# K and V pairs loaded with the two batches on separate partition halves, and three V pairs kept instead of two

## Chip, cores, metric

One core of a Trainium2 chip. The metric is the device time of one execution in microseconds. Executions of one kernel agree within about 1% (the four of the kernel before: 185.68 to 186.6 us). The ratios and intervals are from fast runs in the same rounds on the same chip, so a ratio is not quite that of the medians quoted beside it. A difference counts as faster or slower only when it is clear of 2%.

## The reference

A decode step: one token for each of 4 batches, twice through an attention layer and a gated feed-forward layer, with the same weights and the same cache both times.

```python
x = x + A(layernorm(x)); x = x + B(layernorm(x))     # and both once more

# A: 32 query heads, 8 K/V heads of 128, the last W = 2048 cached positions
q = (x @ wq) per head; scores = q . k * Dh**-0.5; p = softmax(scores); o = p . v; o @ wo
# B: h = sigmoid(x @ w_gate) * (x @ w_up); h @ w_down
```

Everything is bfloat16. The window of K is 16.8 MB (4 batches x 8 heads x 2048 x 128 x 2 bytes), and that of V as much. K stays in on-chip memory for the second attention. V doesn't fit and is read twice, except for what is kept.

## The kernel before

The program is made from a plan: every operation states what it reads and writes, a scheduler orders them, and all transfers from DRAM are issued in order by SyncE. The on-chip arena has 50 slots of 4 KB per partition. A tile is two slots (1 MB): 16 tiles hold all of K, nine are free for V and weights. A "pair" is one head's K or V of two batches. These are the parts that matter (cut):

```python
KEEP_V = cfg.get("KEEP_V", 2)      # V pairs not read again; one of them is parked in PSUM

def pair_d(cache, h, bp):          # the DRAM side of one pair's load: 64 rows, 2 batches, 8 KB
    return cache[2 * bp:2 * bp + 2, h, SK - W:SK, :].rearrange("b (p j) d -> p b (j d)", p=64)

# scores: 32x32 blocks of the K tile are transposed in place by VectorE, so the batch of a
# column is its parity: 16 columns of one batch, every second 4-byte word
kt = kpair(hk, b // 2).rearrange("p (j c x i t) -> p c t i j x", c=2, x=16, i=2, t=2)
pe.matmul(ps[32 * gi:32 * gi + NR, bank, :], qbd[...], kt[:, cp // 2, cp % 2, b % 2, :, :], ...)
```

With this order, partition 2p holds row p of the pair's first batch and partition 2p + 1 that of the second: the batches are interleaved over the partitions.

## Time and profile before

| | before |
|---|---|
| time, median | 186.48 us |
| bytes moved, mean rate | 72.12 MB, 391 GB/s |
| packets' time as a share of 16 DMA engines | 97.2% |
| TensorE busy | 55% |

From the page of the kernel before: the share of DMA busy time in 40 equal slices of the span (9 is 90% or more), the rate in each slice, the packet counts, the main load queue (packets, MB, share of 16 engines), the chain of waits by engine, and two groups of matmuls (line, engine, operation, output <- inputs, shapes, count | busy us, mean ns | idle before, releaser).

```profile
DMA  5999999999999999999999999999999999999980
GB/s 198 425 427 427 425 403 391 411 421 419 409 387 425 419 421 403 392 419 419 400 391 414 412 407 393 403 350 417 330 396 419 419 423 416 418 416 402 412 341 24
DMA packets 15379, 72.12 MB, mean 391 GB/s; under 512 B 1144, under 2 KB 5248, under 8 KB 8704
...
q1 hardware_dynamic: 15352, 71.84, 97.2%
...
DMA 52%; PE 25%; SPq 16%; DVE 4%; issue 2%; ACT 0%
...
L697 PE MATMUL ps<-arena,qbd 128*16 128x512 bf16 x256 | 32.5, 626 | 16.9 <-DVE qbd L668 8.4 <-DVE arena L678 7.5 <-issue 1.0
...
L726 PE MATMUL ps<-prow,perm 64*128 64x256 bf16 x64 | 7.4, 315 | 2.4 <-ACT prow L714 2.3
```

The DMA engines are full from the second slice to the 38th. By this page the kernel is bound by the bytes it reads (experiment 4 shows where that reading ends). One small number is worth more than it seems: "under 512 B 1144". No load of this kernel has rows that short. In the trace they are packets of four bytes. The input x and the output have four data packets each, and with them four of these, one at the end of each data packet (3 or 4 ns before it). The count of all is 71 large loads x 16 + 4 for the four-row output + 4 for the four-row input x = 1144. I read one as the mark of one DMA engine's end of a transfer (an interpretation). Read this way, the page tells how many engines each load used.

The views of single stretches give the second attention (129 to 165 us) 405 GB/s, with a chain of TensorE pieces. TensorE is busy for 33.6 of these 36 us, and the DMA share is 1.01.

### The profile page before, as it was taken

The numbers are of one execution on the slowest core, as the hardware profiler recorded it, in microseconds if no ns is written. First come the engines' busy times: TensorE is split into PE (matmuls) and PEld (weight loads), VectorE is DVE, ScalarE is ACT, GpSimd is POOL, SyncE is SP. The second block draws the span as 40 slices with busy tenths as digits, with TensorE's granted clock in tenths as the row PEclk, the third lists the DMA queues.
The fourth block names the chain that finished last, engine by engine and source line by source line (L and its number), as shares of the span: only waits on it lengthen the run. The fifth ranks groups of instructions, "written<-read, shape, count | busy, mean of one in ns | idle before, by whom it ended". The sixth has DMA issues, their size and how long they took to land.

```text
span 184.4 us, 4421 instructions
## 1 busy us (share of the span) xinstructions
PE 101.2 (55%) x1944; PEld 54.7 (30%) x1944; DVE 89.5 (49%) x221; ACT 35.7 (19%) x100; POOL 14.8 (8%) x77
## 2 busy tenths in 40 slices
PE   0532423652807327173373545445979997994474
PEld 0101000332303323023232441210334653584422
DVE  5209998477592565925621531138463442340330
ACT  2003022240212103011020001001365442220010
POOL 4000000110000101010010000000022111120000
PEclk9999995585766756755555555555897897885569
DMA  5999999999999999999999999999999999999980
GB/s 198 425 427 427 425 403 391 411 421 419 409 387 425 419 421 403 392 419 419 400 391 414 412 407 393 403 350 417 330 396 419 419 423 416 418 416 402 412 341 24
DMA packets 15379, 72.12 MB, mean 391 GB/s; under 512 B 1144, under 2 KB 5248, under 8 KB 8704
## 3 DMA queue, kind: packets, MB, share of 16 engines
q1 hardware_dynamic: 15352, 71.84, 97.2%
q8 instruction: 15, 0.25, 0.5%
q14 instruction: 4, 0.03, 0.0%
q10 hardware_dynamic: 8, 0.00, 0.0%
HBM read 71.83 MB, written 0.00 MB: 390 GB/s over the span
## 4 chain that ended last, share of the span: by engine, by line
DMA 52%; PE 25%; SPq 16%; DVE 4%; issue 2%; ACT 0%
DMA arena<-in_A_v_cache_dram 33%; SPq L382 16%; PE ps L697 11%; DMA arena<-in_B_w_down_dram 9%; PE ps L770 8%; DMA arena<-in_A_wq_dram 5%; DMA arena<-in_B_w_up_dram 5%; PE ps L726 2%; PE ps L794 1%; DVE ps L492 1%; PE ps L626 1%; DVE nmax L705 1%; PE ps L749 1%; PE ps L905 1%; PE ps L852 1%
## 5 line engine op out<-in xcount | busy, mean ns | idle before, releaser
L770 PE MATMUL ps<-ebuf,arena 128*128 128x8 bf16 x1024 | 31.0, 167 | 29.7 <-DMA arena<-in_A_v_cache_dram 22.1
L697 PE MATMUL ps<-arena,qbd 128*16 128x512 bf16 x256 | 32.5, 626 | 16.9 <-DVE qbd L668 8.4
L770 PEld LDWEIGHTS ps<-ebuf,arena 128*128 128x128 bf16 x1024 | 28.8, 101 | 36.3 <-DMA arena<-in_A_v_cache_dram 32.5
L678 DVE STREAM_TRANSPOSE arena<-arena 128x1024 f32<-128x1024 f32 x32 | 37.9, 1219 | 3.3 <-DMA arena<-in_A_k_cache_dram 3.0
L705 DVE TENSOR_REDUCE nmax<-ps 128x1 f32<-128x512 f32 x16 | 11.0, 687 | 26.0 <-PE ps L697 26.0
L714 ACT ACTIVATE prow<-ps,nmax 128x512 bf16<-128x512 f32 x16 | 11.0, 687 | 39.6 <-DVE nmax L711 24.9
L671 ACT COPY qbd<-qrep 32x64 bf16<-32x64 bf16 x32 | 7.7, 241 | 40.9 <-PE ps L697 40.3
L697 PEld LDWEIGHTS ps<-arena,qbd 128*16 128x16 bf16 x256 | 6.1, 97 | 31.3 <-issue 22.0
L739 POOL CAST s<-psm 128x1 bf16<-128x1 f32 x16 | 3.0, 188 | 144.4 <-ACT prow L714 144.4
L778 DVE TENSOR_TENSOR onb<-ps,rinv 128x16 bf16<-128x16 f32 x16 | 2.9, 184 | 21.1 <-PE ps L770 21.1
L626 PE MATMUL ps<-arena,xn 128*4 128x512 bf16 x64 | 7.8, 582 | 7.6 <-DMA arena<-in_A_wq_dram 6.2
L794 PE MATMUL ps<-onb,arena 128*128 128x4 bf16 x256 | 9.1, 166 | 3.1 <-DVE onb L778 3.1
L731 ACT CAST prow<-ps 128x512 bf16<-128x512 f32 x16 | 9.4, 587 | 7.1 <-PE ps L726 7.0
L735 DVE STREAM_TRANSPOSE ebuf<-prow 128x256 f32<-128x256 f32 x16 | 7.0, 437 | 6.7 <-ACT prow L731 6.4
L852 PE MATMUL ps<-arena,xn 128*4 128x448 bf16 x64 | 6.5, 560 | 4.9 <-DVE xn L607 3.1
L794 PEld LDWEIGHTS ps<-onb,arena 128*128 128x128 bf16 x256 | 7.9, 101 | 4.1 <-DVE onb L778 2.8
L726 PE MATMUL ps<-prow,perm 64*128 64x256 bf16 x64 | 7.4, 315 | 2.4 <-ACT prow L714 2.3
L596 ACT ACTIVATE lnv<-lnv 128x4 f32<-128x4 f32 x4 | 0.8, 205 | 34.0 <-DVE lnv L593 34.0
L634 DVE STREAM_TRANSPOSE ebuf<-ps 128x512 f32<-128x512 f32 x4 | 2.9, 715 | 7.7 <-PE ps L626 7.6
L859 DVE STREAM_TRANSPOSE ebuf<-ps 128x448 f32<-128x448 f32 x4 | 2.6, 650 | 7.8 <-PE ps L852 7.8
L668 DVE COPY qbd<-qrep 32x64 bf16<-32x64 bf16 x32 | 5.3, 166 | 0.7 <-ACT qrep L657 0.2
L749 PE MATMUL ps<-sel_b,s 128*128 128x16 bf16 x48 | 3.8, 175 | 3.2 <-POOL s L743 2.4
(61 smaller groups left out, 68.1 us busy)
## 6 DMA issues: line engine op xcount, KB each, us to landing
arena<-in_A_v_cache_dram SPq DMA_DIRECT2D x30, 1024.0 KB, 16.8
arena<-in_A_k_cache_dram SPq DMA_DIRECT2D x16, 1024.0 KB, 16.0
arena<-in_A_wq_dram SPq DMA_DIRECT2D x8, 1024.0 KB, 9.4
arena<-in_A_wo_dram SPq DMA_DIRECT2D x4, 1024.0 KB, 24.3
arena<-in_B_w_gate_dram SPq DMA_DIRECT2D x4, 896.0 KB, 19.7
arena<-in_B_w_up_dram SPq DMA_DIRECT2D x4, 896.0 KB, 15.8
arena<-in_B_w_down_dram SPq DMA_DIRECT2D x2, 1024.0 KB, 12.5
arena<-in_B_w_down_dram SPq DMA_DIRECT2D x1, 768.0 KB, 7.0
```

The source lines that it names most:

```text
L382: o = P.op("sync", name, 0.0, lambda e, dst=dst, src=src: e.dma_start(dst, src), r=r, w=w, dma_bytes=nbytes, dma_rate=tm[rate])
L626: last = pe.matmul(ps[32 * hh:32 * hh + NB, qb, :], xn[:, c * NB:(c + 1) * NB], tile_ap(s)[:, o + hh * 512:o + (hh + 1) * 512], start=(c = ...
L671: P.op("scalar", "qe%s_%d" % (tag, a), c_act(64), lambda s_, dst=dst, src=src: s_.copy(dst, src), r=rd, w=[("q", k2, a)])
L678: P.op("vector", "T%d_%d" % (h, t), c_dve(1024), lambda v, v32=v32: v.transpose(v32, v32), r=[("slot", 4 * h + t)], w=[("slot", 4 * h + t)])
L697: last = pe.matmul(ps[32 * gi:32 * gi + NR, bank, :], qbd[:, q0:q0 + NR], kt[:, cp // 2, cp % 2, b % 2, :, :], start=(cp == 0), stop=(cp = ...
L705: lambda v: v.tensor_reduce(nmax[:, k2:k2 + 1], ps[:, bank, :], AXX, ALU.max),
L714: lambda a: a.activation(prow[:, :].rearrange("p (m x t) -> p m x t", x=16, t=2), ps[:, bank, :].rearrange("p (m t x) -> p m x t", x=16, t ...
L726: last = pe.matmul(ps[:, PBS[i], 0:256], perm[64 * i:64 * i + 64, jh * 128:(jh + 1) * 128], prow[64 * i:64 * i + 64, jh * 256:(jh + 1) * 2 ...
L731: lambda a: a.copy(prow[:, :].rearrange("p (y i t) -> p i y t", i=2, t=2), ps[:, PBS[0]:PBS[0] + 2, 0:256].rearrange("p i (y t) -> p i y t ...
L770: last = pe.matmul(ps[:, ob, bp * 8:bp * 8 + 8], src[:, j * 128:(j + 1) * 128], ev[:, j % 2, j % 16 // 2, x0:x0 + 8], start=(j == 0), stop ...
L794: last = pe.matmul(ps[:, WB, c * NB:(c + 1) * NB], tile_ap(s)[:, o + r_ * D + c * 128:o + r_ * D + (c + 1) * 128], ov[:, r_ * NB:(r_ + 1) ...
L852: last = pe.matmul(ps[32 * g:32 * g + NB, OBS[n], 0:NF], xn[:, c * NB:(c + 1) * NB], tile_ap(s)[:, o:o + NF], start=(c == 0), stop=(c == N ...
```

## The change

The intent: with the batches of a pair on separate partition halves, one score matmul serves both batches (half of the keys at a time) and reads every second bf16 instead of every fourth; the matrices that sort the probabilities become one 128x128 permutation; and a third V pair stays for the second attention, which saves one load of 1 MB. The core of the diff, with cuts marked:

```diff
-    KEEP_V = cfg.get("KEEP_V", 2)
+    KEEP_V = cfg.get("KEEP_V", 3)
 ...
         def pair_d(cache, h, bp):
-            return cache[2 * bp:2 * bp + 2, h, SK - W:SK, :].rearrange("b (p j) d -> p b (j d)", p=64)
+            return cache[2 * bp:2 * bp + 2, h, SK - W:SK, :].rearrange("b (p j) d -> b p (j d)", p=64)
 ...  (scores; still 16 matmuls of 512 columns per head)
-                        kt = kpair(hk, b // 2).rearrange("p (j c x i t) -> p c t i j x", c=2, x=16, i=2, t=2)
+                        kt = kpair(hk, bp).rearrange("p (j c x t) -> p c t j x", c=2, x=32, t=2)
 ...  (the maximum now has to cross the two halves)
+            for g in range(2):
+                P.op("vector", "nx%d%s" % (g, tag), tm["dve_small"],
+                     lambda v, g=g: v.tensor_copy(nmax[64 * g:64 * g + 64, 4 + k2:5 + k2],
+                                                  nmax[64 - 64 * g:128 - 64 * g, k2:k2 + 1]), ...)
 ...  (sorting the probabilities: four matmuls become one)
-                for jh in range(2):
-                    for i in range(2):
-                        last = pe.matmul(ps[:, PBS[i], 0:256], perm[64 * i:64 * i + 64, jh * 128:(jh + 1) * 128],
-                                         prow[64 * i:64 * i + 64, jh * 256:(jh + 1) * 256], ...)
+                 lambda pe: pe.matmul(ps[:, PBS[0], :], perm[:, :], prow[:, :], start=True, stop=True),
 ...  (query copies, masks, selection matrices: adapted to the new layout)
```

More of the change, by code (lines that the diff above doesn't have):

```diff
@@ L321, in build @@
         ebuf = sb("ebuf", [128, 512], F32)
-        qbd = sb("qbd", [128, 2 * NB * 4 * NR], BF16)
+        qbd = sb("qbd", [128, 2 * 2 * 4 * NR], BF16)
         qh = sb("qh", [128, 2 * 64], BF16)
@@ L326, in build @@
         ident_b = sb("ident_b", [128, 128], BF16)
-        perm = sb("perm", [128, 2 * 128], BF16)
+        perm = sb("perm", [128, 128], BF16)
         sel_f = sb("sel_f", [128, NR], F32)
@@ L331, in build @@
         sres = sb("sres", [128, 2], F32)
-        sel_r = sb("sel_r", [128, REP], F32)
+        sel_r = sb("sel_r", [128, 2 * REP], F32)
         maskr = sb("maskr", [128, 32], F32)
         mxt = sb("mxt", [128, 2 * 32], F32)
-        nmax = sb("nmax", [128, 4], F32)
+        nmax = sb("nmax", [128, 6], F32)
         psm = sb("psm", [128, 2], F32)
@@ L524, in build @@
             for bp in range(2):
-                P.op("gpsimd", "perm%d_%d" % (jh, bp), 300.0,
-                     lambda g, jh=jh, bp=bp: g.affine_select(
-                         perm[:, jh * 128:(jh + 1) * 128].rearrange("p (a x) -> p a x", a=4)[
-                             :, :, 16 * jh + 8 * bp:16 * jh + 8 * bp + 8].rearrange("p a (i r) -> p a i r", i=2),
-                         ones_f[:, :].rearrange("p (a i r) -> p a i r", a=4, i=2),
-                         [[-REP, 4], [-64, 2], [-1, REP]], ALU.is_equal, 0.0,
-                         base=-32 * bp, channel_multiplier=1),
-                     r=[("ones_f",), ("perm",)], w=[("perm", jh, bp)])
-        perms = [("perm", jh, bp) for jh in range(2) for bp in range(2)]
+                for i in range(2):
+                    z0 = 16 * jh + 8 * bp + REP * i
+                    P.op("gpsimd", "perm%d_%d_%d" % (jh, bp, i), 200.0,
+                         lambda g, jh=jh, bp=bp, i=i, z0=z0: g.affine_select(
+                             perm[:, 64 * i:64 * i + 64].rearrange("p (y z) -> p y z", y=2)[:, :, z0:z0 + REP],
+                             ones_f[:, 0:2 * REP].rearrange("p (y r) -> p y r", y=2),
+                             [[-REP, 2], [-1, REP]], ALU.is_equal, 0.0,
+                             base=-(64 * jh + 32 * bp + 2 * REP * i), channel_multiplier=1),
+                         r=[("ones_f",), ("perm",)], w=[("perm", jh, bp, i)])
+        perms = [("perm", jh, bp, i) for jh in range(2) for bp in range(2) for i in range(2)]
         P.op("vector", "sel_f", 200.0,
-             lambda v: v.tensor_reduce(sel_f[:, :],
-                                       perm[:, 0:128].rearrange("p (a x) -> p a x", a=4)[:, :, 0:NR].rearrange("p a x -> p x a"),
-                                       AXX, ALU.add),
+             lambda v: v.tensor_reduce(sel_f[:, :], perm[:, :].rearrange("p (g x) -> p x g", x=NR), AXX, ALU.add),
              r=perms, w=[("sel_f",)])
@@ L541, in build @@
         P.op("vector", "sel_r", 100.0,
-             lambda v: v.tensor_reduce(sel_r[:, :], sel_f[:, :].rearrange("p (g r) -> p r g", g=4), AXX, ALU.add),
+             lambda v: v.tensor_reduce(sel_r[:, :], sel_f[:, :].rearrange("p (g y) -> p y g", g=2), AXX, ALU.add),
              r=[("sel_f",)], w=[("sel_r",)])
-        P.op("vector", "maskr", 100.0,
-             lambda v: v.tensor_scalar(maskr[:, :].rearrange("p (y r) -> p y r", r=REP),
-                                       sel_r[:, :].unsqueeze(1).broadcast_to([128, 8, REP]),
-                                       1.0, 1.0e30, ALU.subtract, ALU.mult),
-             r=[("sel_r",)], w=[("maskr",)])
+        P.op("vector", "maskr_z", 100.0, lambda v: v.memset(maskr[:, 16:32], 1.0e30), w=[("maskr_z",)])
+        for i in range(2):
+            P.op("vector", "maskr%d" % i, 100.0,
+                 lambda v, i=i: v.tensor_scalar(maskr[:, 8 * i:8 * i + 8].rearrange("p (y r) -> p y r", r=REP),
+                                                sel_r[:, REP * i:REP * i + REP].unsqueeze(1).broadcast_to([128, 2, REP]),
+                                                1.0, 1.0e30, ALU.subtract, ALU.mult),
+                 r=[("sel_r",)], w=[("maskr", i)])
         o = P.op("scalar", "x_in", 1300.0, lambda e: e.dma_start(x_nat, x_d), w=[("prow",)])
@@ L662, in q_unit @@
             for a in range(4):
-                dst = qbd[32 * a:32 * a + 32, k2 * 256:(k2 + 1) * 256].rearrange(
-                    "p (x y) -> p x y", y=NR)[:, :, a * REP:(a + 1) * REP]
-                src = qrep[32 * a:32 * a + 32, h * 64:(h + 1) * 64].rearrange("p (x r) -> p x r", r=REP)
+                dst = qbd[32 * a:32 * a + 32, k2 * 128:(k2 + 1) * 128].rearrange(
+                    "p (l c y) -> p l c y", l=2, y=NR)[:, :, :, a * REP:(a + 1) * REP]
+                src = qrep[32 * a:32 * a + 32, h * 64:(h + 1) * 64].rearrange(
+                    "p (l i c r) -> p i l c r", l=2, i=2, r=REP)[:, a // 2]
                 rd = [("qrep", h // 4)]
@@ L692, in e_s @@
                 for cp in range(4):
-                    for b in range(NB):
-                        gi = 2 * (b % 2) + b // 2
-                        kt = kpair(hk, b // 2).rearrange("p (j c x i t) -> p c t i j x", c=2, x=16, i=2, t=2)
-                        q0 = ((k2 * NB + b) * 4 + cp) * NR
+                    for gi in range(4):
+                        jh, bp = gi // 2, gi % 2
+                        kt = kpair(hk, bp).rearrange("p (j c x t) -> p c t j x", c=2, x=32, t=2)
+                        q0 = ((k2 * 2 + bp) * 4 + cp) * NR
                         last = pe.matmul(ps[32 * gi:32 * gi + NR, bank, :], qbd[:, q0:q0 + NR],
-                                         kt[:, cp // 2, cp % 2, b % 2, :, :], start=(cp == 0), stop=(cp == 3))
+                                         kt[:, cp // 2, cp % 2, jh * NJ:(jh + 1) * NJ, :], start=(cp == 0), stop=(cp == 3))
                 return last
@@ L706, in softmax_unit @@
                  r=[("pss", k2)], w=[("mx", k2)], banks=(bank,))
+            for g in range(2):
+                P.op("vector", "nx%d%s" % (g, tag), tm["dve_small"],
+                     lambda v, g=g: v.tensor_copy(nmax[64 * g:64 * g + 64, 4 + k2:5 + k2],
+                                                  nmax[64 - 64 * g:128 - 64 * g, k2:k2 + 1]),
+                     r=[("mx", k2)], w=[("nx", k2, g)])
             P.op("vector", "mk" + tag, tm["dve_small"],
-                 lambda v: v.tensor_scalar(mk, maskr[:, :], nmax[:, k2:k2 + 1], None, ALU.add),
-                 r=[("mx", k2), ("maskr",)], w=[("mk", k2)])
+                 lambda v: v.scalar_tensor_tensor(mk, nmax[:, 4 + k2:5 + k2].broadcast_to([128, 32]), nmax[:, k2:k2 + 1],
+                                                  maskr[:, :], ALU.max, ALU.add),
+                 r=[("mx", k2), ("nx", k2, 0), ("nx", k2, 1), ("maskr", 0), ("maskr", 1), ("maskr_z",)], w=[("mk", k2)])
             P.op("vector", "nm" + tag, tm["dve_small"],
@@ L713, in softmax_unit @@
             P.op("scalar", "ex" + tag, c_act(512) + 200.0,
-                 lambda a: a.activation(prow[:, :].rearrange("p (m x t) -> p m x t", x=16, t=2),
-                                        ps[:, bank, :].rearrange("p (m t x) -> p m x t", x=16, t=2), ACTF.Exp, bias=nmax[:, 2 + k2:3 + k2], scale=1.0,
+                 lambda a: a.activation(prow[:, :].rearrange("p (m x t) -> p m x t", x=32, t=2),
+                                        ps[:, bank, :].rearrange("p (m t x) -> p m x t", x=32, t=2), ACTF.Exp, bias=nmax[:, 2 + k2:3 + k2], scale=1.0,
                                         accum_out=psm[:, k2:k2 + 1]),
@@ L721, in turn_p @@
             ob = OBS[k2]
-            def e_pp(pe):
-                last = None
-                for jh in range(2):
-                    for i in range(2):
-                        last = pe.matmul(ps[:, PBS[i], 0:256], perm[64 * i:64 * i + 64, jh * 128:(jh + 1) * 128],
-                                         prow[64 * i:64 * i + 64, jh * 256:(jh + 1) * 256], start=(jh == 0), stop=(jh == 1))
-                return last
-            P.op("tensor", "pp" + tag, tm["pe_sq"], e_pp, r=[("prow",)] + perms, w=[("ppb",)], banks=PBS)
-            P.op("scalar", "pc" + tag, c_act(512),
-                 lambda a: a.copy(prow[:, :].rearrange("p (y i t) -> p i y t", i=2, t=2),
-                                  ps[:, PBS[0]:PBS[0] + 2, 0:256].rearrange("p i (y t) -> p i y t", t=2)),
-                 r=[("ppb",)], w=[("prow",)], banks=PBS)
+            P.op("tensor", "pp" + tag, tm["pe_sq"],
+                 lambda pe: pe.matmul(ps[:, PBS[0], :], perm[:, :], prow[:, :], start=True, stop=True),
+                 r=[("prow",)] + perms, w=[("ppb",)], banks=(PBS[0],))
+            P.op("scalar", "pc" + tag, c_act(512), lambda a: a.copy(prow[:, :], ps[:, PBS[0], :]),
+                 r=[("ppb",)], w=[("prow",)], banks=(PBS[0],))
             P.op("vector", "pt" + tag, c_dve(256),
```

## The prediction

(896 + 61 + 3 + 4 + some 8 = 972 us, put as 970. The 16 engines, and 4 for the load of x, are read from the trace of the kernel before; that an outermost count of 2 gives two engines, always the same, was the author's estimate. The 8 us came from no measurement.)

> **What bounds the kernel now.** HBM traffic. The page gives 72.12 MB at 391 GB/s over 184.4 us; DMA is 9 in nearly all 40 slices, the main queue's packets fill 97.2% of 16 engines' time, and the chain of waits is 52% DMA. TensorE is busy 55%. Only in the second attention (129 to 165 us) is the chain made of TensorE pieces: per head 1.9 us of scores and 1.6 us of PV, while the DMA stays full (405 GB/s).
>
> **What the change does.**
> 1. One more V pair stays: 70 big loads, not 71. 1.05 MB less, at about 415 GB/s some 2.5 us.
> 2. Scores: still 16 matmuls of 512 columns per head, reading every second bf16 instead of every fourth, so perhaps faster (626 ns each now). The permutation falls from four matmuls (315 ns each) to one; the query copies halve; two tiny cross-half copies per head come on VectorE (about 0.17 us each, as its other small operations). Perhaps 5 us less PE work, hidden under the DMA.
> 3. The loads change shape. A pair's DRAM side counted 64 rows, then 2 batches, then 8 KB; now 2 batches, then 64 rows. The SBUF side still counts 128 partitions.
>
> **Step 3 decides.** [...] the 4-row load of x left 4 data packets and 4 four-byte completion packets; the 71 big loads and the 4-row output left 1140 four-byte packets = 71 x 16 + 4. So each K or V load goes from 16 engines to 2, always the same two.
>
> **Cost.** An 8 KB packet has a median of 311 ns in the trace (26.3 GB/s per engine); the last lone engine still moves 2 KB each 80 ns (25.6 GB/s), so being alone doesn't help. A load puts 64 packets on each of two engines: 19.9 us. 16 K and 29 V loads: 896 us. The other 25 loads' packets sum to 984 us, 61 us per engine, queued on the same two. 957 us, plus 3 us before, 4 us after, and some 8 us where slots aren't free between layers: 970 us (an estimate from these durations), all on the critical path. Gains 1 and 2 don't show, except that the kept pair is worth 20 us.
>
> **Prediction.** 970 us, range 890 to 1060. Faster by over 2%: 0.03; within 2%: 0.12; slower: 0.85. If the loads still spread over 16 engines, about 184 us.
>
> **What the profile would show.** Mean rate near 75 GB/s, 71.1 MB; DMA share about a tenth, except where weights load; K and V landing after tens to hundreds of us; four-byte packets on the main queue near 45 x 2 + 25 x 16 + 4 = 494. TensorE idle mostly until K and V loads. The durations of score and permutation matmuls show step 2.
>
> **What would make it wrong.** [...] Two engines running faster when fourteen are idle, or slower because their streams lie 16 MB apart: 880 to 1100 us. Longer idle between layers: tens of us more.

## The result

975.35 us median (973.5 to 976.83, 4 runs) against 186.48 us: 5.233 times the time, interval 5.216 to 5.250. The lines of the page of the kernel after that answer to those above:

```profile
DMA  4111211111121111121111211243511111111153
GB/s 198 53 53 54 87 53 53 54 53 54 53 88 52 54 53 53 53 89 51 53 54 53 89 50 54 82 111 150 197 54 53 54 53 54 53 54 53 53 159 120
DMA packets 14605, 71.07 MB, mean 73 GB/s; under 512 B 498, under 2 KB 4602, under 8 KB 8058
...
q1 hardware_dynamic: 14578, 70.78, 19.4%
...
another core or an unknown queue 39%; DMA 29%; SPq 25%; PE 5%; DVE 0%; issue 0%; ACT 0%; POOL 0%
...
L699 PE MATMUL ps<-arena,qbd 128*16 128x512 bf16 x256 | 29.7, 612 | 157.6 <-DVE arena L680 80.1 <-DVE qbd L670 77.2 <-ACT qbd L673 0.3
...
L731 PE MATMUL ps<-prow,perm 128*128 128x512 bf16 x16 | 9.3, 584 | 2.9 <-ACT prow L722 2.9
```

Three readings. First, the rate is 50 to 54 GB/s, mostly 53 or 54, wherever only K and V load: an eighth of 427, as 2 is an eighth of 16. It rises to 82 or more only where weights load. Second, short packets fell from 1144 to 498 = 45 x 2 + 25 x 16 + 4 + 4, where 45 is the number of K and V loads and 25 that of all others. With 16 for the others, no other number of engines per K or V load fits, and from 800 to 870 us, with V loads alone, the DMA share is 0.13 of 16 engines, that of two. The packets also show that it is always the same two engines: each 1 MB load of wo is 1024 packets of 1 KB, and of each of the four, 896, the share of 14 engines, move first (those of the first load from 108.9 to 113.9 us), while the last 128, the share of two, wait behind K and V (until 132.3 to 135.6 us). Third, the chain now names "another core or an unknown queue" for 39%. Only one core runs; the pieces stand where K and V loads end, and the list of DMA issues gives no landing time for those loads either (nor for some weight loads on 16 engines, wq and w_gate among them). With 4 engines for a load it is 8%, with 8 none. Why the profile can't match these loads isn't shown. The times below say that it is not a new kind of wait.

The view of waits of the kernel after (engine and line that waited, for what: us in total, times, longest) says what TensorE and VectorE wait for:

```profile
PE ps L771 <- DMA arena<-in_A_v_cache_dram: 676.2, 29, 58.7
...
DVE arena L680 <- DMA arena<-in_A_k_cache_dram: 281.4, 16, 20.2
```

And the view of the issuing line shows how long an issue took: for one K or V load (median) SyncE was held for 19.3 us, where it was 0.6 us before. The columns are the count, then the duration in ns (least, median, most) and the first and last start in us.

```profile
L382 SPq DMA_DIRECT2D arena<-in_A_v_cache_dram x29: 506/19343/35879, 108.3 to 887.5; - x29
L382 SPq DMA_DIRECT2D arena<-in_A_k_cache_dram x16: 680/19310/35880, 3.4 to 475.5; - x16
```

That is the time in which SyncE was held, and not all of a load's time. In the second attention a head needs two V loads, and the scores of one head after the other start in the chain at (start us, us, what):

```profile
755.39 1.81 PE ps L699 x11
...
794.77 1.81 PE ps L699 x11
...
834.16 1.81 PE ps L699 x11
```

39.4 us for two loads is 19.7 us each. For the 64 packets of 8 KB that each of two engines gets, that is 308 ns a packet, or 26.6 GB/s for each engine.

### The profile page after: what moved, and what is told of

Same layout as the page of the kernel before. It is cut to its first block, busy times and chain, and to the rows that moved or that the text cites. A ratio compares the mean times of both kernels' runs of the same rounds, so it can differ in the third digit from the quotient of the medians.

```text
span 975.1 us, 4362 instructions
## 1 busy us (share of the span) xinstructions
PE 104.3 (11%) x1896; PEld 56.0 (6%) x1896; DVE 96.1 (10%) x255; ACT 35.1 (4%) x100; POOL 14.8 (2%) x81
## 4 chain that ended last, share of the span: by engine, by line
another core or an unknown queue 39%; DMA 29%; SPq 25%; PE 5%; DVE 0%; issue 0%; ACT 0%; POOL 0%
SPq L382 25%; DMA arena<-in_A_v_cache_dram 23%; DMA arena<-in_B_w_down_dram 3%; DMA arena<-in_B_w_up_dram 3%; PE ps L771 2%; PE ps L699 1%; DMA arena<-in_A_wq_dram 1%; PE ps L906 0%; PE ps L795 0%; ACT prow L722 0%; PE ps L627 0%; PE ps L750 0%; PE ps L731 0%; DVE ps L492 0%
## 5 line engine op out<-in xcount | busy, mean ns | idle before, releaser
L699 PE MATMUL ps<-arena,qbd 128*16 128x512 bf16 x256 | 29.7, 612 | 157.6 <-DVE arena L680 80.1
L673 ACT COPY qbd<-qrep 32x32 bf16<-32x32 bf16 x32 | 6.9, 216 | 250.8 <-PE ps L699 250.2
L731 PE MATMUL ps<-prow,perm 128*128 128x512 bf16 x16 | 9.3, 584 | 2.9 <-ACT prow L722 2.9
L757 DVE RECIPROCAL rinv<-ps 128x16 f32<-128x16 f32 x16 | 3.8, 240 | 34.5 <-PE ps L750 34.3
L492 DVE STREAM_TRANSPOSE ps<-arena 128x512 f32<-128x512 f32 x4 | 2.6, 702 | 39.5 <-DMA arena<-in_A_v_cache_dram 39.5
L670 DVE COPY qbd<-qrep 32x32 bf16<-32x32 bf16 x32 | 5.2, 161 | 0.7
L711 DVE COPY nmax<-nmax 64x1 f32<-64x1 f32 x32 | 4.7, 147 | 1.0
```

What stands on the lines that cost most here:

```text
L673: P.op("scalar", "qe%s_%d" % (tag, a), c_act(64), lambda s_, dst=dst, src=src: s_.copy(dst, src), r=rd, w=[("q", k2, a)])
L699: last = pe.matmul(ps[32 * gi:32 * gi + NR, bank, :], qbd[:, q0:q0 + NR], kt[:, cp // 2, cp % 2, jh * NJ:(jh + 1) * NJ, :], start=(cp == 0 ...
L731: lambda pe: pe.matmul(ps[:, PBS[0], :], perm[:, :], prow[:, :], start=True, stop=True),
```

## The experiments

Eleven kernels ran. Several put K and V on other partitions than the arithmetic expects, so that they compute something else than the reference. They were all reported correct. By the scales of the inputs in the reference (an estimate), the scores are of the order of 0.003, so that each query averages some 2048 values of nearly equal weight, and attention adds about 0.00006 to an x of about 0.05. The comparison doesn't see which values it got. So "correct" is no evidence for those runs; they are marked as wrong and used for their time alone. Nor is it evidence for the others: that they put K and V in the right place follows from their code and not from the check.

### 1. The load's shape by itself, and everything but the load's shape

Theory: the load's shape is the whole loss. Rival: the rest of the change takes part in it. The kernel before with one line of the change (wrong):

```diff
-            ... .rearrange("b (p j) d -> p b (j d)", p=64)
+            ... .rearrange("b (p j) d -> b p (j d)", p=64)
```

> The kernel before with only the loads of the kernel after (2 batches outermost); WRONG RESULT on purpose. Theory: 46 loads x 64 packets x 0.310 us on the same two engines, one load more than after, so 975 + 20 = 995 us and 46 x 2 + 25 x 16 + 4 = 496 four-byte packets. Rival: if the loss needs the rest of the change, much less.

Measured: 994.08 us (2 runs), 500 short packets (496 and the 4 of x).

```profile
DMA packets 14735, 72.12 MB, mean 73 GB/s; under 512 B 500, under 2 KB 4604, under 8 KB 8060
```

One line of the diff makes the whole loss. The run is 18.7 us longer than the full change, about the 19.7 us of the one V load that the change saves.

The reverse, the kernel after with that one line put back (wrong):

> The kernel after with the loads of the kernel before (64 rows outermost, batches interleaved over the partitions); WRONG RESULT on purpose, all instructions and all bytes of the change are there. Theory (the load's outermost count of 2 costs everything): 183 to 185 us, 1136-type four-byte packets again (70 x 16 + 4 = 1124). Rival (something else of the change, the new matmul patterns or the kept pair, takes part in the loss): clearly over 190 us. The difference to the run with KEEP_V = 3 alone is the worth of the reworked scores and permutation: theory says under 1 us, since they are hidden under the DMA.

Measured: 187.47 us against 186.92 us, ratio 1.006 (1.0004 to 1.012). The loss is gone. But the 183 to 185 us that I had expected is not there. Neither is the prediction's "about 184 us" for the case that the loads still spread. Experiment 4 follows that up.

### 2. Is it the number of engines, or where the two streams lie in DRAM?

The two streams of a load lie 16 MB apart in DRAM. A rival says that they meet in the same part of the DRAM and slow each other. So the same shape was tried with two neighbouring heads of one batch (2 MB apart), and the outermost count was set to 4 (batches) and 8 (heads); all read the same bytes in all, and all are wrong:

```diff
-  cache[2 * bp:2 * bp + 2, h, ...].rearrange("b (p j) d -> p b (j d)", p=64)
+  cache[2 * bp + h % 2, h // 2 * 2:h // 2 * 2 + 2, ...].rearrange("n (p j) d -> n p (j d)", p=64)   # two_heads
+  cache[:, h, <half of the window>, :].rearrange("b (p j) d -> b p (j d)", p=32)                     # four
+  cache[h // 2, :, <quarter of the window>, :].rearrange("n (p j) d -> n p (j d)", p=16)             # eight
```

(Theory B of four and eight is an estimate: that the engines of one load slow each other, so that an 8 KB packet takes up to twice the 311 ns; in both it allowed for times between those of A and B. No run had shown such a slowing.)

> The kernel before with loads of 2 outermost x 64 rows x 8 KB, but the two streams of a load come from neighbouring heads of one batch, 2 MB apart in DRAM, not from two batches 16 MB apart; the same bytes in all, WRONG RESULT on purpose. Theory (the count decides): 995 us as in the run with two batches outermost, 496 four-byte packets. Rival (the two streams 16 MB apart meet in the same part of DRAM and slow each other): clearly faster, packets under 309 ns.

> The kernel before with loads of 4 outermost (all batches) x 32 rows x 8 KB; the same bytes, WRONG RESULT on purpose. 46 x 4 + 25 x 16 + 4 = 588 four-byte packets. Theory A (only the number of engines counts): 46 x 32 x 0.31 = 456 us, plus 61 for the other loads and 16: 533 us. Theory B [...]: packets of about 620 ns and up to 990 us [...].

> The kernel before with loads of 8 outermost (all heads) x 16 rows x 8 KB; the same bytes, WRONG RESULT on purpose. 46 x 8 + 25 x 16 + 4 = 772 four-byte packets. Theory A (engines only): 46 x 16 x 0.31 = 228 us, plus 61 and some 12: 301 us. Theory B [...]: packets of about 620 ns, about 530 us[...].

| outermost count | time, us | short packets | mean time of an 8 KB packet, ns |
|---|---|---|---|
| 64 (before) | 186 | 1144 | 319 |
| 2 batches, 16 MB apart (batch_first) | 994.08 | 500 | 320 |
| 2 heads, 2 MB apart | 994.60 | 500 | 320 |
| 4 batches | 555.28 | 592 | 332 |
| 8 heads | 349.7 (the one fast run; the slow one 355.55) | 776 | 378 |

(The means are of all 8 KB packets, with the 768 of weight loads.) 16 MB or 2 MB between the streams gives the same time, so that rival is out. The time follows the count, and the short packets are those of as many engines for a K or V load as the count says (46 x 2, 46 x 4 and 46 x 8, with 25 x 16 + 4 + 4), each time to the packet. With 4 and 8 the times are above those of theory A (533 and 301) and far below those of theory B (990 and 530). (The profile with 8 is of its slow run.) At least half of the packets still take 309 to 312 ns; most of the others take up to twice that. The slow ones (over 500 ns) come in stretches. With 4 engines 85% of them lie within 2 us of a packet of a weight load, and where K and V load alone (166 to 222 us) the mean is 310 ns. With 8 it is 67%; K and V alone took a mean of 478 ns from 35.4 to 53 us, but 310 ns from 274 to 292 us. So much of the excess goes with weight loads that move beside K and V. What slowed the packets in the stretch at 35 us isn't shown.

### 3. Can the halves be had with all 16 engines?

The kernel after, each pair loaded by two transfers, one batch to one half, the right result:

```diff
+        def dma_pair(name, dst, srcs, w):       # srcs: the two batches, 64 rows of 8 KB each
+            first = dma(name + "a", dst[0:64, :], srcs[0], w=w, rate="bw_8k")
+            first.twin = P.op("sync", name + "b", 0.0, lambda e, d=dst[64:128, :], s_=srcs[1]: e.dma_start(d, s_), ...)
```

(Readers of the tile wait for a load and for its twin.)

(The 215 GB/s is about half of the 427 of the best slices of the kernel before.)

> The kernel after with each pair loaded by two transfers of 64 partitions, one per batch (outermost count 64 on both sides), right result. Theory A (only the number of engines counts): all 16 engines work, about 184 to 188 us, 90 x 16 + 25 x 16 + 4 = 1844 four-byte packets. Theory B [...]: 47 MB at about 215 GB/s, 220 us, plus 60 us for the rest and 10 us: about 290 us, with 8 KB packets of about twice 311 ns.

Measured: 291.93 us against 186.92 us, ratio 1.561 (1.555 to 1.568). All 16 engines take part (1848 short packets) and look busy throughout, and still the rate is half:

```profile
DMA  7999999999999999999999999689999999999993
GB/s 275 374 223 222 217 249 241 219 219 223 224 242 219 224 220 224 216 242 222 233 232 230 222 225 225 263 298 406 314 215 217 219 217 222 216 220 214 293 414 119
DMA packets 15956, 71.08 MB, mean 243 GB/s; under 512 B 1848, under 2 KB 5952, under 8 KB 9408
```

An 8 KB packet now takes 595 ns (median), not 311. The slices with K and V alone show 214 to 233 GB/s, most of them under 226, about half of the 427 of the best slices before.

Three runs test whether the partitions written are the cause, or something else, all on the kernel before and all with the right result. The first has transfers like those of the run with halves (one pair more, as only two V pairs are kept), but they write even and odd partitions. The second has the interleaved reads of before, but writes halves. The third is a control for the number and size of the transfers.

```diff
+  dst[0:128:2, :] <- batch 0,           dst[1:128:2, :] <- batch 1               # split_even
+  dst[0:64, :]    <- rows 0:32 of both, dst[64:128, :]  <- rows 32:64 of both    # split_part
+  dst[:, 0:SLOT]  <- first 4 KB of each row, dst[:, SLOT:] <- the other 4 KB     # split_cols
```

(The theory is that the partitions written decide.)

> The kernel before with each pair loaded by two transfers, one per batch, as in the run with halves: the same DRAM reads, the same sizes and count, 64 partitions each; but the first writes the even partitions 0, 2 to 126 and the second the odd ones. Right result. Theory [...]: 186 to 190 us, 8 KB packets at 309 to 320 ns. Rival (64-partition transfers, or reading one batch's 512 KB by all engines at once, are slow by themselves): about 290 us, packets near 600 ns.

> The kernel before with each pair loaded by two transfers: 32 rows of both batches to partitions 0 to 63, the other 32 rows to 64 to 127. Right result; the DRAM reads are those of the kernel before, the partitions those of the run with halves. Theory [...]: about 292 us, packets near 600 ns. Rival (reading one batch at a time from DRAM was the slow part): 186 to 190 us.

> The kernel before with each pair loaded by two transfers of 128 partitions x 4 KB (column halves). Right result. A control for the doubled number of transfers and their half size: theory 187 to 193 us (a 4 KB packet took 159 ns against 311 for 8 KB, 2% more per byte). If this is far slower, the number of transfers is part of the loss with halves.

| run | time, us | ratio to before | median 8 KB packet, ns |
|---|---|---|---|
| split_even | 189.20 | 1.019 (1.003 to 1.035) | 309 |
| split_part | 293.77 | 1.582 (1.552 to 1.612) | 589 |
| split_cols | 191.88 | 1.033 (1.018 to 1.048) | 4 KB pieces: 159 |

The rate rows of split_even, then of split_part:

```profile
GB/s 196 430 425 422 420 407 397 418 413 423 392 404 420 417 422 388 410 422 418 378 419 413 405 400 404 354 419 402 359 404 423 425 420 420 416 405 406 390 35 1
```

```profile
GB/s 277 374 220 220 221 248 237 223 221 226 219 242 221 227 226 222 213 246 227 232 230 229 222 227 249 327 350 370 267 227 222 229 221 228 226 227 229 281 412 117
```

The partitions written decide, not the reads, the size or the number of transfers. (By the 2% rule split_even and split_cols, with two runs each, are unclear: a loss of some per cent from twice the transfers is likely, but it is far from the 58% of split_part.) Writing 64 partitions at a time is no problem when they are the even or the odd ones (309 ns a packet); writing only the lower or only the upper 64 is (589 ns). Why isn't shown; the runs show the partitions. So with these loads the layout of the change costs either 14 of the 16 engines (one transfer, 53 or 54 GB/s with K and V alone) or half of the rate (two transfers, 214 to 233 GB/s). The interleaving of the kernel before avoids both. A third way to load it wasn't tried.

### 4. Where did the saved megabyte go?

> The kernel before with KEEP_V = 3 and nothing else. Traffic falls by 1.05 MB; at the 415 GB/s of the trace that is 2.5 us, so 184 us if the DMA stays as full as before (theory: HBM traffic bounds it). Rival: one slot fewer for loads ahead of their use during the first feed-forward part makes the DMA wait, and the time stays at 186 or grows.

Measured: 187.03 us against 186.92 us, ratio 0.9998 (0.994 to 1.006). Here the rival was right: nothing is gained. The profile shows where the gain went. In stretches of 5 us around the feed-forward layer between the two attentions (times, then busy us and count of PE, PEld, DVE, ACT and POOL, granted clock, DMA share, GB/s), first the kernel before:

```profile
110.00:115.00 5.00, 2.58 (x24) 0.52 (x24) 0.82 (x2) 1.09 (x5) 0.00 (x0) 0.50 1.00 392
...
130.00:135.00 5.00, 4.50 (x64) 1.68 (x60) 3.25 (x12) 2.33 (x7) 0.76 (x4) 0.96 1.03 344
```

Then with KEEP_V = 3 alone:

```profile
110.00:115.00 5.00, 2.58 (x24) 0.52 (x24) 0.82 (x2) 1.14 (x5) 0.00 (x0) 0.50 0.73 242
...
130.00:135.00 5.00, 4.49 (x56) 1.25 (x56) 3.19 (x10) 1.60 (x7) 0.00 (x0) 0.87 0.86 280
```

(392 - 242) GB/s x 5 us + (344 - 280) GB/s x 5 us = 1.07 MB that is not moved in these ten microseconds, as much as the 1.05 MB that the kept pair saves. The kept pair holds a tile, so one fewer is free for weights ahead of their use. SyncE's waits, of the kernel before and then with KEEP_V = 3, show it: the line that issues loads waits longer for the gate and up matmuls, which free the tiles.

```profile
SPq L382 <- PE ps L852: 8.7, 4, 5.5
```

```profile
SPq L382 <- PE ps L852: 12.5, 4, 7.9
```

The last load in the chain of waits comes much earlier, too. These pieces (start us, us, what) are the last loads of the two chains, of the kernel before and then of keep3:

```profile
165.35 15.77 DMA arena<-in_B_w_down_dram
```

```profile
125.46 6.84 DMA arena<-in_A_wq_dram
```

After 132 us the chain of keep3 names only computing: bytes saved after that help nobody. The first scores of the second attention start 3.8 us later in it than in the chain of the kernel before (132.95 against 129.19 us), and the end comes 1 us earlier (spans of 183.4 and 184.4 us).

The profiled run of keep3 was the fastest of its four (185.12 us), so it doesn't overstate the stall. A tile more, which would give the stall back, needs 8 KB more per partition, and such a kernel doesn't build: with NS = 52 the build of the kernel before stops with "need 212992B, have 212863B" for the arena. So no version of this that beats the kernel before was found.

The last part, the reworked scores and permutation without the third pair (interleaved loads, wrong):

> The kernel after with interleaved loads and KEEP_V = 2: only the reworked scores, permutation and masks differ from the kernel before; WRONG RESULT on purpose. Theory (before is bound by the DMA except within the second attention, and the rework is hidden): 186 to 187.5 us, the same as before, with PE about 8 us less busy. Rival (the rework lengthens the chain from head to head in the second attention by its two copies on VectorE and that shows): 188 us or more. Rival 2 (less PE work shows): 184 or less.

Measured: 186.63 us against 185.98 us, ratio 1.004 (0.998 to 1.011). The rework is worth nothing that these runs resolve. The "8 us less" of TensorE in that expectation was my misreading: I took it from the profile of rows_first (92.8 us), where records were missing. Its permutation group counted 1 matmul of 16. The groups of this run have them all:

```profile
L699 PE MATMUL ps<-arena,qbd 128*16 128x512 bf16 x256 | 29.3, 605 | 15.4 <-DVE qbd L670 8.9 <-DVE arena L680 6.4
...
L731 PE MATMUL ps<-prow,perm 128*128 128x512 bf16 x16 | 9.5, 594 | 7.7 <-ACT prow L722 7.7
```

Scores took 3.2 us less TensorE time than before (29.3 against 32.5), the permutation 2.1 us more (9.5 against 7.4): the 64 smaller matmuls overlapped (64 x 315 ns is 20.2 us, in 7.4 us of busy time), the 16 large ones did not (16 x 594 ns is 9.5 us). TensorE is busy for 101.6 us, against 101.2 before. And the new copies across the halves sit in the chain from head to head: in the chain of rows_first, between one head's scores and the next, these are some of the pieces (start us, us, what):

```profile
152.45 1.92 PE ps L699 x16
...
154.39 0.69 DVE nmax L707
...
155.28 0.15 DVE nmax L711
...
155.46 0.15 DVE nmax L711
...
156.43 0.79 ACT prow L722 x2
```

From 152.45 to the next head's scores at 157.80 it is 5.35 us, through VectorE and ScalarE. In the kernel before it was 4.45 us at this place (149.49 to 153.94), on TensorE alone; but this is its shortest step. The mean of four heads in a row is 5.30 us in rows_first (141.75 to 162.95) and 5.04 us before (139.78 to 159.93), a loss of about 0.3 us a head. Whether this costs time in the whole kernel, the runs don't settle: rows_first and keep3 both lie within 0.7% of the kernel before.

## Why the prediction was right, point by point

- **The number of engines.** Predicted 2 engines for each K or V load and 494 four-byte packets on the main queue; the trace has 494. With outermost counts of 2, 4 and 8 the short packets (500, 592, 776) are those of 2, 4 and 8 engines for a K or V load, and with 64 (1144) those of 16, each to the packet. What had made it credible before any run was the four-row load of x, with its 4 data packets and 4 four-byte packets.
- **The time.** Predicted 970 us, measured 975.35. The agreement is better than its terms. A load took 19.7 us where I had 19.9, as packets follow each other every 308 ns (a packet takes 309 to 311). That is about 10 us less over 45 loads. All the rest took about 89 us (975 - 45 x 19.7), not 76. The two errors nearly cancel, which is luck. Where those 13 us lie isn't settled. The 8 us for missing slots between layers were no measured term: gaps of over 0.5 us in the whole queue add up to 3.6 us, 3.0 of them just before the output is written, but for 7 us more only one packet was under way, so that at least one of the two engines stood idle.
- **Lone engines aren't faster.** Predicted from the tail of the trace (2 KB each 80 ns, 25.6 GB/s); 53 GB/s for two engines confirms it, and the same time at 2 MB and at 16 MB (994.60 and 994.08 us) shows no sign that the streams disturb each other.
- **The kept pair.** "Worth 20 us" in the slow kernel: 18.7 us between batch_first and the change. "2.5 us" in a kernel with full rate: nothing. The step that failed is "1.05 MB less, at about 415 GB/s some 2.5 us": it priced the bytes and not the tile that they hold. So "about 184 us" as the time with loads over 16 engines was wrong as well; it is 187.5.
- **"Perhaps 5 us less PE work"** was mis-sized: it is 0.4 us more. Fewer matmuls isn't less time when the many overlapped (the permutation: 64 in 7.4 us, 16 in 9.5). A score matmul that reads every second instead of every fourth element was only 3% shorter (605 against 626 ns; the groups' busy time fell by 10%), and as the granted clocks of the two profiles differ (0.88 and 0.70), even this isn't surely the reading's. That it doesn't show in the time was right.
- **Landing times** of tens to hundreds of us couldn't be checked in the list of issues, which gives none for these loads. The chain puts five stretches of 39 to 47 us down to V loads.

## What to carry to other kernels

Before changing the order of dimensions in a load, look at its outermost count on the DRAM side: in these runs it decided how many DMA engines work (2, 4, 8 or 16: 994, 555, 350 and 186 us). Then look at which partitions one transfer writes: here one half of them took twice the time (589 and 595 ns for an 8 KB packet), every second one did not (309). Both can be read from a profile without a new run, from the count of the four-byte packets and from the time of one data packet. And price what is kept on chip with the tile that it occupies: where the DMA is full because loads run ahead, a tile fewer can give the saved bytes back as a stall (here 1.07 MB were not moved in two stretches of 5 us, against 1.05 MB saved).
